# A fixed order table for every engine, input loads in one queue, more zero matmuls at the start, and three key tiles computed without the folded weight

## The chip, the cores and the metric

The kernel runs on one core of a Trainium2 chip. The metric is the device time of one execution in microseconds; smaller is better. The engines are PE (matrix multiply, with its weight loads listed as PEld), DVE (vector), ACT (scalar), POOL (GpSimd) and SP (which here only issues DMAs). All of them work through their own instruction lists in program order and wait for each other by semaphores.

## The reference

A sequence of 2048 tokens of 512 numbers passes through two layers. Each layer is a linear attention with 32 heads of 16 numbers, and then a gated two-matrix block (GLU) with 1376 hidden columns; both have a residual and a layer norm without weights in front, and the two layers use the same weights. Cut to what matters:

```python
q, k, v = split(x @ wqkv)                       # 32 heads x 16
pq, pk = q @ w_phi, k @ w_phi                   # per head, 16 x 16
phi = concat(softmax(p), softmax(-p))           # for q and for k: 32 features
kv, z = sum_s phi_k * v, sum_s phi_k            # per head, over all tokens
o = (phi_q @ kv) / (phi_q @ z + 1e-6);  x = x + o @ wo
gate, up = xn @ W_gate, xn @ W_up
x = x + (gate * (gate > 0) * up) @ W_down
```

The sums kv and z run over all tokens, so every key of a layer must be done before most queries of it can be used.

## The kernel before, in words

The tokens are 16 tiles of 128 rows in four chunks of four tiles. All of X, all weights and all intermediate tiles stay on the chip.

Setup (lines 201 to 292) issues the loads. On SP's queue: the key part of wqkv, X tile 1, X tiles 2 and 3, the value part. On ACT's queue: X tile 0, w_phi, X tiles 4 to 7, 8 to 11, the query part of wqkv, X tiles 12 to 15. Then it makes constants on DVE and POOL.

The rest is a plan. Each helper calls `pl.op(engine, cost, function, reads, writes, ...)`, which only records an operation; at the end `order` gives every operation a place and a buffer, and `emit` issues them in that order. Before, `order` is a list scheduler: a simulated clock, costs and due times (X_IN, WK_IN and so on), and for each group a rank from the table RANK decide which ready operation each engine takes next.

The operations that the change and the prediction touch:

- `wake` (line 312): STEP["wake"] zero matmuls of 512 columns on PE (line 318).
- `feature_weights` (line 322): Wblk is w_phi spread into a block-diagonal matrix (line 327, DVE). The key weight is folded with it: 16 transposes of wkv by PE (line 351), copies out of PSUM, 16 matmuls against Wblk (line 364), copies into Wk2 (`evacuate`, line 307 on ACT or 309 on DVE). The query weight is folded in the same way from DMA transposes (line 337). So keys in feature form are one product of the normalised tile with Wk2, four matmuls of 512 columns.
- `Norm` (line 370): statistics on DVE (lines 388 and 390), the inverse root on POOL (lines 396 and 398, and 446 and 448 where ACT normalises), the normalised tile on ACT (line 460), DVE or POOL (line 472), and then its transpose, which PE or a DMA of SP makes. STEP["turn"] = "A-AA" has tiles 0, 2 and 3 of the first chunk transposed by PE (line 481), and tile 1 by a DMA (line 490). Two tiles that share one DMA transpose are line 486.
- `keys_values` (line 697): keys (line 710), their two exponentials (line 715, ACT), values (line 663), sums of features per head (`feature_sums`: line 682 both signs at once on DVE, line 692 one sign, or line 679 a first addition of halves on POOL and line 688 the rest on DVE), the reciprocal (line 724), the scaling (line 730, a cut in eighths between POOL and DVE), and the sums over tokens (line 752).
- `queries` (line 781) and `attention` (line 821) do the same for queries (lines 794, 798, 682 to 692, 803, 807, 814) and the output projection (line 884).
- `glu` (line 575): the last 96 hidden columns (line 593), gate and up (line 613), their evacuation (619, 623, 626, 630), and down (line 645). A chunk is cut in parts of its four tiles by STEP["part0"] and ["part1"].
- `load_weights` (line 294): the weights of the projection and the GLU, on SP's queue (line 300).

The strings of STEP give for each tile which engine or variant is used.

Of the kernel before, what the change touches and what calls it, by code (L numbers as in the profile page):

```python
# [8 lines left out]
P = 128  # L9
D = 512  # L10
# [3 lines left out]
NDB = D // P  # L14
# [36 lines left out]
TAIL = {"PE": 0.165, "ACT": 0.12, "DVE": 0.115, "POOL": 0.045, "SP": 0.0}  # L51
SAME = {"PE": -0.165, "ACT": 0.035, "DVE": 0.035, "POOL": 0.08, "SP": 0.0}
HOPS = {("DVE", "POOL"): 0.09, ("ACT", "POOL"): 0.15}
NEXT = {"PE": 0.055, "SP": 0.03}
FREE = 0.06


def hop(a, b):
    return SAME[a] if a == b else HOPS.get((a, b), NEXT.get(b, 0.04))


class Plan:
# [10 lines left out]
    def op(self, eng, occ, fn, reads=(), writes=(), holds=(), lat=0.0, at=0.0, group=None, port=False, long=False):  # L73

        o = Op()
        o.eng, o.occ, o.cost, o.fn, o.lat, o.at, o.port, o.long = eng, occ, occ + TAIL[eng], fn, lat, at, port, long
        o.group, o.i_in = group or self.group
        base, slope = RANK.get(f"{o.group}.{eng}") or RANK[o.group]
        o.bias = base - slope * o.i_in
        o.preds, o.succs, o.i = set(), [], len(self.ops)  # L80
# [18 lines left out]
    def order(self):  # L99
        for o in self.ops:  # L100
            for p in o.preds:
                p.succs.append(o)
        for o in reversed(self.ops):
            o.rank = o.cost + o.lat + max([s.rank + hop(o.eng, s.eng) for s in o.succs], default=0.0)
        free = {k: [0.0] * n for k, (pool, n) in self.kinds.items()}
        engines = sorted({o.eng for o in self.ops})
        busy = {e: 0.0 for e in engines}
        ready = {e: [] for e in engines}
        for o in self.ops:
            o.wait, o.t0 = len(o.preds), o.at  # L110
            if not o.wait:
                ready[o.eng].append(o)
        seq, left, now, shut = [], len(self.ops), 0.0, 0.0
        while left:
            moved, later = False, []
            for e in engines:
                if busy[e] > now + 1e-9:
                    later.append(busy[e])
                    continue
                best = None  # L120
                for o in ready[e]:
                    if o.t0 > now + 1e-9:
                        later.append(o.t0)
                        continue
                    if o.port and shut > now + 1e-9:
                        later.append(shut)
                        continue
# [881 lines left out]
```

## Time and profile before

| what | value |
|---|---|
| median of the runs | 382.15 us (380.12 to 382.57, 3 runs) |
| profiled execution | 380.91 us, of it 379.2 us span |
| granted TensorE clock | 0.999 |
| HBM read, written | 8.44 MB, 2.10 MB |

A row of a group gives line, engine, operation, tile written and read, shape and count, then busy time in us and mean ns of one instruction, then the idle time of the engine just before and what ended it. A row in order of time gives start, duration, engine and line; PE's busy time of matmuls is modelled, and matmuls overlap, so the time of a run of equal matmuls divided by their number is their real pace, not the mean of one. Rows of DMA issues give the queue, KB of each and the us from issue to landing.

### The profile page before, as it was taken

What the parts mean: (1) busy time and instruction counts of PE and PEld (TensorE: products, weight loads), DVE (VectorE), ACT (ScalarE), POOL (GpSimd) and SP (SyncE); (2) the same over time, 40 slices, a digit from 0 to 9 for tenths busy, and PEclk for the clock granted to TensorE, in tenths of its full rate; (3) what the DMA queues carried; (4) which work ended last, traced back from release to release, by engine and by line L of the source; (5) the groups of instructions that cost most, each with busy time, mean ns of one, the idle gap of its engine ahead of it and who ended that gap; (6) DMA issues with size and microseconds to landing.
All of it is one profiled execution on the core that took longest, in us unless ns stands there. A gap on an engine that the chain in (4) does not pass through costs nothing.

```text
span 379.2 us, 6724 instructions
## 1 busy us (share of the span) xinstructions
PE 363.6 (96%) x2380; PEld 189.9 (50%) x2409; DVE 268.0 (71%) x608; ACT 205.5 (54%) x439; POOL 121.1 (32%) x203
## 2 busy tenths in 40 slices
PE   4898999999899999999999999999999999999996
PEld 2444545756445444444444456475654445454444
DVE  4999999999925442763497998999962675172433
ACT  4898979776762446737706925865234135514100
POOL 3798965131110220560155681724310002000000
PEclk9999999999999999999999999999999999999999
DMA  8889936788950230021013070478930075000011
GB/s 262 239 143 227 260 44 144 133 149 146 145 107 2 42 58 15 0 30 27 0 22 77 9 119 3 87 127 146 171 85 14 5 146 115 14 0 16 1 55 57
DMA packets 98882, 32.61 MB, mean 86 GB/s; under 512 B 90560, under 2 KB 98336, under 8 KB 98848
## 3 DMA queue, kind: packets, MB, share of 16 engines
q1 hardware_dynamic: 97216, 29.93, 39.7%
q10 hardware_dynamic: 1632, 2.24, 1.8%
q8 instruction: 19, 0.31, 0.4%
q14 instruction: 15, 0.12, 0.1%
HBM read 8.44 MB, written 2.10 MB: 28 GB/s over the span
## 4 chain that ended last, share of the span: by engine, by line
PE 64%; DVE 24%; DMA 6%; issue 2%; ACT 1%; POOL 1%; SPq 0%; POOLq 0%; ACTq 0%
PE ps L613 37%; PE ps L645 14%; PE ps L884 5%; DMA b<-b 4%; DVE sk L682 4%; DVE rk L724 3%; DVE bnst L388 3%; PE ps L794 3%; PE ps L593 3%; DVE sk L692 2%; DVE b L730 2%; PE q L833 2%; DMA X<-in_A_x_dram 2%; DVE sq L682 1%; DVE sk L688 1%
## 5 line engine op out<-in xcount | busy, mean ns | idle before, releaser
L613 PE MATMUL ps<-b,wu 128*128 128x512 bf16 (+2 forms) x400 | 79.2, 336 | 0.6 <-DMA b<-b 0.6
L613 PE MATMUL ps<-b,wg 128*128 128x512 bf16 (+2 forms) x400 | 78.6, 336 | 0.0
L645 PE MATMUL ps<-wd,b 128*128 128x512 bf16 (+3 forms) x368 | 78.1, 366 | 0.3
L623 ACT ACTIVATE b<-ps 128x512 bf16<-128x512 f32 (+2 forms) x100 | 50.5, 520 | 39.6 <-PE ps L613 39.1
L626 DVE SCALAR_TENSOR_TENSOR b<-ps,b 128x512 bf16<-128x512 f32 (+2 forms) x60 | 35.1, 598 | 39.9 <-PE ps L613 38.9
L645 PEld LDWEIGHTS <-b 128*128 128x128 bf16 (+1 forms) x374 | 35.3, 98 | 39.1
L613 PEld LDWEIGHTS <-wg 128*128 128x128 bf16 x400 | 36.1, 98 | 33.1
L613 PEld LDWEIGHTS <-wu 128*128 128x128 bf16 x400 | 36.2, 98 | 32.7 <-issue 0.9
L730 POOL TENSOR_TENSOR b<-b,rk 128x1024 bf16<-128x1024 bf16 (+6 forms) x28 | 37.5, 1351 | 9.6 <-DVE rk L724 7.9
L798 ACT ACTIVATE b<-ps 128x512 bf16<-128x512 f32 x64 | 33.0, 638 | 5.7 <-PE ps L794 5.1
L715 ACT ACTIVATE b<-ps 128x512 bf16<-128x512 f32 x64 | 33.7, 628 | 1.3 <-PE ps L710 1.3
L679 POOL TENSOR_TENSOR b<-b 128x256 f32<-128x256 bf16 x30 | 19.7, 670 | 43.9 <-ACT b L715 34.1
L570 DVE SCALAR_TENSOR_TENSOR X<-ps,r,X 128x512 bf16<-128x512 f32 (+2 forms) x26 | 18.2, 701 | 20.2 <-PE ps L645 20.1
L710 PE MATMUL ps<-Wk,b 128*128 128x512 bf16 x123 | 29.4, 379 | 2.0 <-DMA b<-b 1.2
L884 PE MATMUL ps<-wo,b 128*128 128x512 bf16 x118 | 29.7, 379 | 1.5 <-DMA b<-b 0.9
L630 DVE TENSOR_TENSOR b<-b,b 128x512 bf16<-128x512 bf16 (+2 forms) x40 | 13.5, 348 | 24.0 <-ACT b L623 22.3
L552 POOL TENSOR_SCALAR ve<-tot 128x4 f32<-128x4 f32 x8 | 1.9, 233 | 88.8 <-ACT sq L548 88.8
L663 PE MATMUL ps<-wkv,b 128*128 128x512 bf16 x122 | 29.9, 386 | 0.3
L794 PE MATMUL ps<-Wq,b 128*128 128x512 bf16 x126 | 29.5, 379 | 0.1
L548 ACT ACTIVATE sq<-b 128x512 bf16<-128x512 bf16 x32 | 20.1, 627 | 17.4 <-DVE b L527 17.0
L598 ACT CAST ur<-ps 128x192 bf16<-128x192 f32 (+1 forms) x18 | 5.4, 302 | 32.2 <-PE ps L593 32.1
L814 POOL TENSOR_TENSOR b<-b,rq 128x512 bf16<-128x512 bf16 x19 | 20.2, 1061 | 8.4 <-DVE rq L807 6.1
(94 smaller groups left out, 493.7 us busy)
## 6 DMA issues: line engine op xcount, KB each, us to landing
out_dram<-X SPq DMA_DIRECT2D x15, 128.0 KB, 1.8
X<-in_A_x_dram ACTq DMA_DIRECT2D x3, 512.0 KB, 7.2
b<-b SPq DMA_TRANSPOSE x94, 3.2
wg<-in_B_W_gate_dram SPq DMA_DIRECT2D x8, 160.0 KB, 3.2
wu<-in_B_W_up_dram SPq DMA_DIRECT2D x8, 160.0 KB, 4.0
wd<-in_B_W_down_dram SPq DMA_DIRECT2D x5, 256.0 KB, 4.7
wkv<-in_A_wqkv_dram SPq DMA_DIRECT2D x2, 512.0 KB, 7.1
wq<-in_A_wqkv_dram ACTq DMA_DIRECT2D x1, 512.0 KB, 8.3
```

The costliest lines, as they stand in the source:

```text
L613: nc.tensor.matmul(ps[:], lhsT=wt[:, b, f * P:(f + 1) * P], rhs=xnT[:, lo:hi, b, :], start=(b == 0), stop=(b == NDB - 1))
L623: pl.op("ACT", 0.045 + 0.43 * share, lambda ups=ups, ru=ru, sign=1.0 if fuse else -1.0: nc.scalar.activation(out=ru[:], in_=ups[:], func=A ...
L626: pl.op("DVE", 0.06 + 0.548 * share, lambda gps=gps, ru=ru, h=h, cs=cs: nc.vector.scalar_tensor_tensor(out=h[:, cs], in0=gps[:], scalar=0. ...
L645: nc.tensor.matmul(yps[:], lhsT=hs[f][:fsz, ti * P:(ti + 1) * P], rhs=st.wd[:fsz, f, cols], start=(f == 0), stop=(f == NFT - 1))
L663: nc.tensor.matmul(vp[:], lhsT=xnT[:, ti, kb, :], rhs=st.wkv[:, kb, D:2 * D], start=(kb == 0), stop=(kb == NDB - 1))
L710: nc.tensor.matmul(ps[:], lhsT=xnT[:, ti, kb, :], rhs=w(kb), start=(kb == 0), stop=(kb == NDB - 1))
L715: pl.op("ACT", 0.48, lambda s=s, ek=ek, pk=pk: nc.scalar.activation(out=ek[:, :, s, :], in_=pk[:].rearrange("p (j x) -> p j x", j=8), func ...
L730: eng.tensor_tensor(out=phiK[:, lo:hi, :, :].rearrange("p j s (f h) -> p (j s) f h", h=4), in0=ek[:, lo:hi, :, :].rearrange("p j s (f h) - ...
L794: nc.tensor.matmul(pq[:], lhsT=xnT[:, ti, kb, :], rhs=st.Wq2[:, kb, :], start=(kb == 0), stop=(kb == NDB - 1))
L798: pl.op("ACT", 0.48, lambda s=s, eq=eq, pq=pq: nc.scalar.activation(out=eq[:, :, s, :], in_=pq[:].rearrange("p (j x) -> p j x", j=8), func ...
L814: (nc.vector if on_dve else nc.gpsimd).tensor_tensor(out=e, in0=e, in1=rq[:].unsqueeze(2).to_broadcast([P, 8, DH, 4]), op=Alu.mult)
L884: nc.tensor.matmul(yps[:], lhsT=turned(b), rhs=st.wo[:, b, :], start=(b == 0), stop=(b == NDB - 1))
```

## The change

Six things change together.

1. The list scheduler, its constants and RANK go. `order` takes the operations in the order of a table ORDER of 1912 numbers (operation numbers in program order) and gives each buffer the free slot that was used longest ago. Due times and costs that stay in the calls no longer decide anything.
2. The loads: SP issues X tile 0, X tile 1, the key weight, X tiles 2 and 3, the value weight, X tiles 4 to 7, 8 to 11, the query weight, X tiles 12 to 15, in this order; ACT issues only w_phi. The code of `load_weights` differs only in a planning number.
3. Zero matmuls: 26 and not 3. In ORDER 14 of them are PE's first work; 8 stand between weight transposes and folds, and 4 among the first raw keys.
4. Keys of tiles 0, 1 and 2 of layer 0 are computed in two steps: the transposed keys from the unfolded weight (16 matmuls of 128 columns), a copy out of PSUM to bf16 (ACT, ACT, DVE for the three tiles), and then four matmuls of 128 columns against Wblk. The other tiles keep Wk2.
5. STEP is new as a whole: turn is "----" (no tile of the first chunk is transposed by PE), and the choices of engine for normalising, sums, scaling, evacuation, transposes and parts differ for most tiles.
6. With this the order on every engine differs throughout.

```diff
-WF_IN, WK_IN, WV_IN, WQ_IN, LOADED = 3.4, 4.2, 6.7, 10.4, 11.0
+LOAD_SP = ((0, 1), (1, 2), "k", (2, 4), "v", (4, 8), (8, 12), "q", (12, 16))
+LOAD_ACT = ("f",)
...
+        owner = {k: [None] * n for k, (pool, n) in self.kinds.items()}
+        last = {k: [-1] * n for k, (pool, n) in self.kinds.items()}
+        self.seq = [self.ops[i] for i in ORDER]
+        for at, o in enumerate(self.seq):
...
+            for b in o.bufs:
+                if b.slot is None:
+                    free = [i for i, u in enumerate(owner[b.kind]) if u is None or not u.left]
+                    b.slot = min(free, key=lambda i: last[b.kind][i])
+                    owner[b.kind][b.slot] = b
...
+        if L == "0" and t < STEP["raw"]:
+            kT, kTs = Buf("ps", [P, NDB, P], F32), Buf("b1", [P, NDB, P], BF16)
+
+            def raw(kT=kT, ti=ti):
+                for b in range(NDB):
+                    for kb in range(NDB):
+                        nc.tensor.matmul(kT[:, b, :], lhsT=st.wkv[:, kb, b * P:(b + 1) * P], rhs=xnT[:, ti, kb, :],
+                                         start=(kb == 0), stop=(kb == NDB - 1))
+            pl.op("PE", 16 * TR, raw, reads=[(xnT, ti)], writes=[(kT, 0)], holds=(kTs,), at=WK_IN)
+            evacuate(st, STEP["kev"][t], lambda kT=kT, kTs=kTs: (kTs[:], kT[:]), 0.59, reads=[(kT, 0)], writes=[(kTs, 0)])
+
+            def features(pk=pk, kTs=kTs):
+                for b in range(NDB):
+                    nc.tensor.matmul(pk[:, b * P:(b + 1) * P], lhsT=kTs[:, b, :], rhs=st.Wblk[:, b, :], start=True, stop=True)
+            pl.op("PE", 4 * TR, features, reads=[(kTs, 0), ("Wblk", 0), ("Wblk", 1)], writes=[(pk, 0)], holds=(ek, phiK))
+        else:
...
-    "part0": "4111", "part1": "6111", "tB0": "D---", "tB1": "--DA", "tA": "----", "wev": "ADADAAAAADDAAAAA",
-    "xn1": "ADAADDAPDAADDAAA", "turn": "A-AA", "wake": 3, "fuse0": "AFAA", "fuse1": "FFFF", "gate": 1, "sA": 2,
...
-    "kr0": "11H11HH11H2211H1", "kr1": "H22P11H2111222PP", "qr0": "21H1H11P2PH11212", "qr1": "112H121HH1HPP12P",
+    "raw": 3, "kev": "AADA", "part0": "3111", "part1": "6111", "tB0": "D--D", "tB1": "A--A", "tA": "----",
+    "wev": "AAAAAAAADDADAAAA", "xn1": "ADAPDAADDAAPAAAA", "turn": "----", "wake": 26, "fuse0": "AFFF",
...
+    "om0": "12222222", "om1": "11222222", "ev0": "AAAAAAAAAAAAAAAA", "ev1": "ADDAAADAAAAAADDA",
+    "ks0": "6087550655660860", "ks1": "4661026302258586", "kr0": "2H2P11H11PP21HP1", "kr1": "222PH11P1P1HP112",
```

The first numbers of ORDER are `0 1 2 3 4 5 127 125 134 149 143 140 123 150 141 133 144 142 139 131 129 137 159 8 9`: the statistics and POOL steps of tile 0, then zero matmuls (123 to 148), the two halves of Wblk (149, 150), the first weight transposes (159) and tile 1 (8, 9).

More of the change, by code (lines that the diff above doesn't have):

```diff
@@ L99, in order @@
     def order(self):
[L100 to L112, printed above, removed]
@@ L317, in wake @@
         z = Buf("ps", [P, D], F32)
[L318 removed]
+        pl.op("PE", 0.2155, lambda z=z: nc.tensor.matmul(z[:], lhsT=st.zero[:, 0:P], rhs=st.zero[:], start=True, stop=True),
               writes=[(z, 0)], at=1.2)
```

156 lines of the change are left out of this document (44 added, 112 removed), and 103 rows, old and new, of tables (ORDER, RANK, STEP).

## The prediction

> **What bounds the kernel now.** I read the page first (busy shares and the chain), then busy time by stretches, then the start in order of time.
>
> ```profile
> PE 363.6 (96%) x2380; PEld 189.9 (50%) x2409; DVE 268.0 (71%) x608; ACT 205.5 (54%) x439; POOL 121.1 (32%) x203
> ...
> PE 64%; DVE 24%; DMA 6%; issue 2%; ACT 1%; POOL 1%; SPq 0%; POOLq 0%; ACTq 0%
> ```
>
> PE is nearly always busy and holds 64% of the chain that ended last; DVE holds 24%. The stretches tell where each is true (columns: stretch and length, then busy us of PE, PEld, DVE, ACT, POOL, granted clock, DMA share, GB/s).
>
> ```profile
> 0.00:12.00 12.00, 6.17 (x42) 4.01 (x42) 7.18 (x26) 5.64 (x10) 4.83 (x21) 1.00 0.87 285
> 12.00:60.00 48.00, 45.20 (x330) 22.72 (x337) 48.00 (x100) 43.32 (x85) 40.70 (x55) 1.00 0.77 173
> 60.00:184.00 124.00, 122.03 (x783) 64.29 (x790) 79.92 (x205) 77.09 (x178) 27.79 (x50) 1.00 0.40 71
> 184.00:250.00 66.00, 64.82 (x476) 33.75 (x482) 59.71 (x122) 40.22 (x85) 34.42 (x58) 1.00 0.29 53
> 250.00:350.00 100.00, 99.11 (x617) 52.18 (x620) 62.31 (x142) 37.45 (x83) 13.38 (x21) 1.00 0.39 75
> ```
>
> The first 12 us are a start: PE idles 5.8 us and DVE 4.8. From 12 to 60 DVE has no idle time at all, with PE at 94%, ACT at 90% and POOL at 85%: everything is nearly full and DVE sets the pace. From 60 to 350 PE is the bound and idles 2.0 + 1.2 + 0.9 = 4.0 us in all. So the change can win only at the start, by freeing DVE up to 60, or from those 4 us.
>
> **The start, PE.**
>
> ```profile
> 1.24 1.46 PE L318 MATMUL ps<-zero 128*128 128x512 bf16 x3 [1.24 <-DVE zero L234]
> 5.37 1.89 PE L351 MATMUL ps<-ident,wkv 128*128 128x128 bf16 x16 [2.66 <-DMA wkv<-in_A_wqkv_dram]
> 7.11 1.01 PE L364 MATMUL ps<-Wblk,b 128*128 128x128 bf16 x8
> 10.04 0.61 PE L364 MATMUL ps<-Wblk,b 128*128 128x128 bf16 x4 [1.93 <-DVE b L309]
> 12.00 1.80 PE L663 MATMUL ps<-wkv,b 128*128 128x512 bf16 x4
> 13.63 1.89 PE L710 MATMUL ps<-Wk,b 128*128 128x512 bf16 x7
> ...
> 66.93 0.67 PE ps L613 x12
> ...
> 322.25 16.40 PE ps L613 x76
> ```
>
> The last two rows are the later rate: 56 ns for a pass of 128 columns, 216 ns for 512. The early rows run at about half of it: 118 ns for 128 columns at 5.37, 450 ns for 512 at 12.00, 270 at 13.63. The first work on a token tile is the values matmul at 12.00.
>
> **When the first tile reaches PE afterwards.** This is the step on which the sum turns. The order table, decoded by numbering the operations in program order, puts on PE 14 zero matmuls, then the 16 weight transposes and folds among 8 more zeros, and then the raw keys of tile 0, which wait for that tile transposed. Before, tiles 0, 2 and 3 are transposed by PE (turn "A-AA"); now all go through the DMA queue of SP (turn "----"), and on that queue nine loads stand ahead of them.
>
> ```profile
> 3.86 0.69 DVE L388 BATCH_NORM_STATS2 bnst<-X 128x6 f32<-128x512 bf16 x1 [1.09 <-DMA X<-in_A_x_dram]
> 6.48 0.17 DVE L390 BATCH_NORM_AGGREGATE mv<-bnst 128x2 f32<-128x6 f32 x1
> 8.21 0.82 ACT L460 ACTIVATE b<-X,ve,rstd 128x512 bf16<-128x512 bf16 x1
> 5.34 0.33 ACTq L240 DMA_DIRECT2D X<-in_A_x_dram  x1
> X<-in_A_x_dram ACTq DMA_DIRECT2D x1, 128.0 KB, 3.0
> X<-in_A_x_dram ACTq DMA_DIRECT2D x1, 512.0 KB, 8.1
> ```
>
> (The last two rows are DMA issues with the us from issue to landing.) Tile 0 landed after 3.0 us, at 3.8. From the start of the aggregate to the end of the normalising it is 9.03 - 6.48 = 2.55 us, and the statistics take 0.69. With X first in its row and the aggregate no longer behind the wait for w_phi, the normalised tile stands at about 3.8 + 0.7 + 2.55 = 7.0 us. The nine loads need an issue of 0.45 us each and are all issued by about 5.5, so the transpose is issued behind them at 7. The bytes are the same as before, whose last load landed at 5.34 + 8.1 = 13.4; I take 13.4 again (12.4 if one row is freer of small pieces, 14.6 if one queue is slower than two). Does a transpose pass loads that are ahead of it in its queue?
>
> ```profile
> 17.93 0.43 SPq L300 DMA_DIRECT2D wr<-in_B_W_gate_dram  x1
> 18.95 1.23 SPq L486 DMA_TRANSPOSE b<-b  x1
> wr<-in_B_W_gate_dram SPq DMA_DIRECT2D x1, 96.0 KB, 2.9
> b<-b SPq DMA_TRANSPOSE x1, 4.8
> 34.03 1.23 SPq L337 DMA_TRANSPOSE b<-wq  x1
> wu<-in_B_W_up_dram SPq DMA_DIRECT2D x1, 160.0 KB, 4.0
> b<-wq SPq DMA_TRANSPOSE x1, 4.5
> DMA to landing us min/median/max: 2.7/3.1/4.8
> ```
>
> The transpose at 18.95 follows loads whose last landed at 17.93 + 2.9 = 20.8, and took 4.8 us where the median is 3.1; the one at 34.03 follows a burst of loads (landing in 4.0) and took 4.5. In the two places shown where loads are ahead in the queue the transpose lands after them. Before, the large X parts and wq came through ACT's queue and SP's was nearly empty at 10.7. So I take the first transposed tile 0.9 us behind the last load (a median transpose less its issue and half its tail), at 14.3. The Trainium skill, DMA: Bandwidth & Descriptors, section on queues, rings and completion order, says that each DMA engine consumes the descriptors of a ring in order and that SP and ACT own one row each. By that rule the 14.3 is firm; the traces agree as far as the two places go.
>
> **The sum, against the profiled execution's own 380.9 us** (span 379.2 and 1.7 around it; the median of the runs shown is 382.15, its lowest 380.12).
>
> 1. First tile on PE at 14.3 and not 12.00: +2.3. The same shows on DVE: its table puts the copy of tile 2's raw keys out of PSUM (L309) ahead of the first sum of features. PE reaches the end of those raw keys after three raw tiles, two values and one feature step, 14.3 + 1.9 + 1.8 + 0.4 + 0.9 + 0.9 + 0.9 = 21.1 (half rate for the first 4 us, by the rows at 5.37 and 12.00), so the first sum comes at 21.7 against 19.6 before. That is +2.1, one delay and not two. Take +2.3; bounds -2.8 (tile at 9.2, first rival) and +3.5.
> 2. PE's own work. Three raw tiles cost 16 + 4 passes of 56 ns in place of 4 of 216: +0.25 each, +0.75. Three PE transposes in the first chunk go: -0.67. Later three more attention tiles and one more centred tile are transposed by PE (4 x 4 x 56 ns = +0.9), and chunk 0 of the first GLU is cut in three parts and not two. The 80 further passes cost only their fixed part, by the two rates (4 x 56 - 216) / 3 = 2.7 ns each: +0.2. Together +1.2, all in stages where PE is 94% to 99% busy.
> 3. The 23 added zero matmuls lie in PE's idle time until 8.5 and before raw keys that wait: 0. If the cover goes (tile 0 at 9.2), the four zeros left behind them cost 4 x 0.22 = 0.9.
> 4. Three raw tiles add three copies out of PSUM, two on ACT and one on DVE; ACT loses three copies of turned tiles and gains two of weights: nothing, in ACT's 4.7 idle us.
> 5. DVE up to 100 us.
>
> ```profile
> L682 DVE TENSOR_REDUCE sk<-b 128x64 f32<-128x1024 bf16 x9 | 10.5, 1188 | 0.0
> L688 DVE TENSOR_REDUCE sk<-b 128x32 f32<-128x256 f32 x5 | 2.7, 547 | 0.0
> L472 DVE TENSOR_SCALAR b<-X,mv,rstd 128x512 bf16<-128x512 bf16 x6 | 2.6, 450 | 0.0
> L730 DVE TENSOR_TENSOR b<-b,rk 128x1024 bf16<-128x1024 bf16 x2 | 1.4, 680 | 0.0
> L692 DVE TENSOR_REDUCE sq<-b 128x32 f32<-128x512 bf16 x21 | 13.5, 659 | 0.0
> L814 DVE TENSOR_TENSOR b<-b,rq 128x512 bf16<-128x512 bf16 x13 | 5.7, 445 | 0.2 <-POOL rq L807 0.2
> L679 POOL TENSOR_TENSOR b<-b 128x256 f32<-128x256 bf16 x11 | 7.2, 666 | 1.7 <-ACT b L798 1.4 <-ACT b L715 0.3
> L472 POOL TENSOR_SCALAR b<-X,mv,rstd 128x512 bf16<-128x512 bf16 x1 | 2.1, 2092 | 0.1
> ```
>
> By the new strings of STEP, the keys of layer 0 have six full sums and not nine (-3.5), eleven half sums and not five (+3.2), two normalisings fewer (-0.9), eight more eighths of a scaling (+0.7), two bf16 copies fewer and one f32 copy more (about 0): -0.5. The queries of layer 0 have four full sums fewer (-4.7), five single ones (+3.3) and three half ones more (+1.6), five scalings fewer (-2.2): -2.0. Together -2.5 on the engine that sets the pace; I take -2.0, since part of the queries' share lies behind 60, where PE is the bound. Bounds -2.5 and 0.
> 6. The order past 60. PE idles 4.0 us there, mostly behind transposes. A fixed table can fit them better or worse; no row shows which. Bounds -4.0 and +4.0; I take -2.0, since the new DVE and ACT shares leave the transposes' inputs earlier in the first GLU. What is late next is PE itself.
>
> Sum: +2.3 + 1.2 - 2.0 - 2.0 = -0.5, so 380.9 - 0.5 = 380.4.
>
> The clock at 14.3 is one more unknown. The row at 12.00 shows half rate after a broken start; afterwards PE works from 1.24 to about 9 and then waits 5 us. The Trainium skill, TensorE: Matmul & The Clock Gate, part 1, says that about 3.4 us of idling bring the half rate back. By that rule the zeros warm nothing that lasts, and the sum stays; if PE stayed warm, the first 4 us would be done in 2, and the sum would be 378.4. No row of this trace has a warm PE idle that long.
>
> **The rivals.**
> (a) The transposes are not held up by the loads, and tile 0 is on PE at 7.0 + 2.2 = 9.2. For it: nothing in the first 12 us shows a transpose at all, so the two places above are small cases. Then DVE idles about 3.2 us at the start (until X lands, and for the next parts) where the forecast has 4.8 + 2.1 = 6.9: -3.7, and PE gains 5.1. With 0.9 for the zeros: between 375.3 + 0.9 and 376.7, say 376.
> (b) Slower: POOL becomes the bound of the keys. It is busy 40.7 us of 48 from 12 to 60. It gets six more half-sum additions (6 x 0.67 = 4.0) and a second normalising of 2.1, and loses eight eighths of a scaling (2.0): +4.1, in a stage that starts 2 us later. It decides if more than half of POOL's 7.3 idle us there stay waits; then the stage lengthens by about 4.1 and nothing of step 5 is won: 380.4 + 2.0 + 4.1 = 386.5. Against it: POOL's order is new too, and may wait less.
> (c) The start is as forecast, but the table takes out nearly all of the 4.0 us of PE's idling past 60 and more of DVE's: 380.9 + 2.3 + 1.2 - 2.5 - 4.0 = 377.9.
>
> **How the numbers follow.** Forecast 0.48, its own range 378 to 384; (a) 0.27; (b) 0.15; (c) 0.10. Range 374 to 386.5: (a) with 2 us of margin below, (b)'s price above. A measurement of this kernel can tell about 1% from no change; that is below 378.3 or above 386.0 against 382.15. Faster: most of (a), 0.24, 0.07 of (c), 0.04 of the forecast: 0.35. Slower: 0.10 of (b) and 0.03 of the forecast: 0.13. Within 1%: 0.52.
>
> **What would show it.** Step 1: the first 128-column matmul of raw keys near 14.3, behind a wait for a DMA, and the first transposes of SP with landings of 5 us or more; near 9 it is (a). Step 5: DVE's busy time from 12 to 60 still 48, its first sum near 21.7. Rival (b): waits of PE or DVE for POOL's scaling of keys. Step 6: PE's idle time from 60 to 350 against 4.0. The prediction is wrong if the first tile is early, or if the later order loses by waits what no row here can show.

## The result and the profile after

The kernel after takes 394.41 us (median of 4 runs, 393.69 to 394.76) against 382.36 us for the kernel before beside it: a ratio of 1.032, with a 95% interval of 1.027 to 1.037. The forecast was 380.4, with a range up to 386.5; it was wrong in sign and outside its range. The profiled execution spans 392.8 us, 13.6 more than before. Single executions of 779 to 1381 us (one of the kernel before, one each of two kernels below) are left out of all ratios.

First the same stretches of the kernel after from 12 us on, in the columns used above (stretch, length, busy us of PE, PEld, DVE, ACT, POOL, granted clock, DMA share, GB/s):

```profile
12.00:60.00 48.00, 40.58 (x319) 22.82 (x325) 43.03 (x81) 37.68 (x72) 35.79 (x49) 0.93 0.64 133
60.00:184.00 124.00, 119.22 (x863) 67.20 (x875) 101.05 (x243) 69.95 (x181) 44.41 (x69) 1.00 0.46 86
184.00:250.00 66.00, 63.77 (x411) 31.66 (x415) 48.76 (x88) 28.83 (x54) 28.68 (x47) 1.00 0.23 39
250.00:350.00 100.00, 98.68 (x671) 53.76 (x680) 64.24 (x158) 54.35 (x135) 20.44 (x32) 1.00 0.46 82
```

From 12 to 60 every engine now idles more: PE 7.4 us (before 2.8), DVE 5.0 (0), ACT 10.3 (4.7), POOL 12.2 (7.3), and the clock is 0.93. From 60 to 350 PE idles 8.3 us where it idled 4.0. DVE's idle time lies nearly all in one place, ahead of its first sum of features, where it waits for PE's raw keys of tile 2; the second row is the stretch from that sum to the end of the keys of layer 0:

```profile
23.29 0.69 DVE L239 CAST b<-ps 128x512 bf16<-128x512 f32 x1 [4.21 <-PE ps L648]
```

```profile
23.90:66.07 42.17, 36.18 (x284) 18.76 (x287) 41.41 (x70) 34.10 (x67) 33.54 (x36) 1.00 0.58 127
```

There DVE is busy 41.4 of 42.2 us: it still sets the pace, and PE, ACT and POOL wait.

Where the delay arises is told by fixed places of the program. R is built (before L774, after L720) once the last keys of a layer are summed. These are the rows by line of the kernel before and of the kernel after (duration min/median/max in ns, then the first and the last start in us):

```profile
L774 DVE TENSOR_TENSOR R<-M,q x4: 427/430/439, 52.9 to 233.4; 128x272 bf16<-128x272 bf16 x4
```

```profile
L720 DVE TENSOR_TENSOR R<-M,q x4: 373/424/439, 66.1 to 247.1; 128x272 bf16<-128x272 bf16 x4
```

R of layer 0 is 13.2 us late, R of layer 1 is 13.7 us late, and the span is 13.6 us longer. The whole loss is made before 66 us, in the start and the keys of layer 0; from R on the kernel takes 326.7 us, and 326.3 before. That stage divides at the first sum of features on DVE, at 19.53 before and 23.90 after: 4.4 us are lost ahead of it and 8.8 behind it. Not all of the 8.8 is waiting: the table also does 31 query matmuls ahead of R (7.5 us of PE) where the kernel before did 19 (4.4 us).

The start of the kernel after, PE in order of time, SP's DMA issues, and the us from issue to landing of the last load and of the first transpose:

```profile
10.08 0.83 PE L294 MATMUL ps<-Wblk,b 128*128 128x128 bf16 x8
15.33 1.89 PE L648 MATMUL ps<-b,wkv 128*128 128x128 bf16 x16 [4.42 <-DMA b<-b]
```

```profile
5.31 0.57 SPq L161 DMA_DIRECT2D X<-in_A_x_dram  x1
6.78 7.93 SPq L420 DMA_TRANSPOSE b<-b  x4
```

```profile
X<-in_A_x_dram SPq DMA_DIRECT2D x1, 512.0 KB, 9.5
b<-b SPq DMA_TRANSPOSE x1, 8.5
```

The first transpose is issued at 6.78 and lands 8.5 us later, at 15.3, 0.5 us behind the last load (5.31 + 9.5 = 14.8). PE stands still for 4.4 us, and what it does then goes at half rate (118 ns for each of the 16 passes of 128 columns). The clock, by stretches:

```profile
13.00:14.00 1.00, 0.00 (x0) 0.00 (x0) 1.00 (x3) 0.00 (x0) 0.84 (x4) 0.82 2.37 125
14.00:15.00 1.00, 0.00 (x0) 0.00 (x0) 1.00 (x7) 0.00 (x0) 0.90 (x3) 0.50 0.60 113
```

A mean of 0.82 puts the fall to 0.50 near 13.6, 2.7 us after PE's last matmul ended at 10.9.

Behind the first sum the trace shows something that I had not looked for. The groups of DVE from 15 to 66, scalings of keys and sums:

```profile
L612 DVE TENSOR_REDUCE sk<-b 128x64 f32<-128x1024 bf16 x6 | 7.1, 1181 | 0.0
L618 DVE TENSOR_REDUCE sk<-b 128x32 f32<-128x256 f32 x11 | 6.2, 589 | 0.0
L676 DVE TENSOR_TENSOR b<-b,rk 128x1024 bf16<-128x1024 bf16 x4 | 5.3, 1317 | 0.0
L676 DVE TENSOR_TENSOR b<-b,rk 128x384 bf16<-128x384 bf16 x4 | 3.6, 894 | 0.0
L676 DVE TENSOR_TENSOR b<-b,rk 128x256 bf16<-128x256 bf16 x5 | 2.8, 560 | 0.0
```

The full sums last as long as before (1181 against 1188 ns). A whole scaling (128x1024) takes 1317 ns where the same shape took 680, and 128x256 takes 560. In order of time, DVE first and POOL second:

```profile
47.02 1.38 DVE L676 TENSOR_TENSOR b<-b,rk 128x256 bf16<-128x256 bf16 x1
49.36 0.40 DVE L676 TENSOR_TENSOR b<-b,rk 128x384 bf16<-128x384 bf16 x1
55.51 0.22 DVE L676 TENSOR_TENSOR b<-b,rk 128x256 bf16<-128x256 bf16 x1
56.18 1.94 DVE L676 TENSOR_TENSOR b<-b,rk 128x1024 bf16<-128x1024 bf16 x1
```

```profile
46.98 1.26 POOL L676 TENSOR_TENSOR b<-b,rk 128x640 bf16<-128x640 bf16 x1
55.66 1.91 POOL L676 TENSOR_TENSOR b<-b,rk 128x1024 bf16<-128x1024 bf16 x1 [0.69 <-DVE rk L670]
```

At 47.02 a scaling of 128x256 starts on DVE just after POOL has begun its part of the same tile, and ends 0.16 us after POOL's (48.40 against 48.24); 128x256 with POOL idle, at 55.51, takes 0.22. At 56.18 the same: DVE ends at 58.12, POOL at 57.57. So DVE's scaling does not get on in earnest until POOL's has ended. With 0.68, 0.40 and 0.22 us alone, the 13 scalings of the three shapes would take 4 x 0.68 + 4 x 0.40 + 5 x 0.22 = 5.4 us; they take 11.7. These 6.3 us lie on the engine that paced this stage. POOL waits behind them for DVE's reciprocals, and PE for the scaled keys (us in total, times, longest):

```profile
POOL b L676 <- DVE rk L670: 7.3, 4, 2.4
...
PE q L698 <- DVE b L676: 4.1, 6, 1.5
...
PE q L698 <- POOL b L676: 1.6, 1, 1.6
```

The Trainium skill, SBUF — State Buffer, section on who interferes with whom, calls the pair of ports that DVE shares with GpSimd an exclusive lock: a DVE instruction with two SBUF inputs contends with a GpSimd instruction that reads SBUF, the order of issue decides which of them blocks, and a reduction of DVE never contends. The rows agree: DVE's scaling at 47.02, begun 0.04 us behind POOL's, waits for it, and the full sums keep their length.

Both parts of one tile's scaling wait for the same reciprocal, so they become ready together: a cut scaling collides almost by design unless something keeps the parts apart. The list scheduler had such a rule (by its simulated clock, a `port` operation of DVE is not started while a `long` operation of POOL runs; the variable `shut` in the code before). The table has no rule. The kernel before cuts ten of the 16 tiles of layer 0 as well (`ks0` = "7877011827873780"), so it is not the cutting that is new.

So two causes were proposed, each with rivals: the late first tile (held up by SP's queue, or by the DMA engines being full whatever the queue), and DVE's scalings (held up by POOL, or POOL simply being the bound, or the raw keys, or the zeros, or the order as such).

### The profile page after: what moved, and what is told of

Its sections match the earlier page's. It is cut to its first block, busy times and chain, and to the rows that moved or that the text cites. A ratio compares the mean times of both kernels' runs of the same rounds, so it can differ in the third digit from the quotient of the medians.

```text
span 392.8 us, 6991 instructions
## 1 busy us (share of the span) xinstructions
PE 371.6 (95%) x2529; PEld 200.0 (51%) x2564; DVE 276.6 (70%) x615; ACT 211.5 (54%) x477; POOL 134.9 (34%) x216
## 4 chain that ended last, share of the span: by engine, by line
PE 65%; DVE 27%; DMA 3%; issue 2%; ACT 1%; POOL 1%; DVEq 0%; POOLq 0%; ACTq 0%
PE ps L543 31%; PE ps L575 16%; PE ps L830 5%; DVE b L676 4%; DMA b<-b 3%; DVE sk L612 3%; DVE sq L622 3%; PE ps L523 3%; PE ps L640 2%; DVE rk L670 2%; DVE sk L618 2%; DVE sq L618 2%; DVE sk L622 2%; PE ps L248 2%; DVE b L799 2%
## 5 line engine op out<-in xcount | busy, mean ns | idle before, releaser
L553 ACT ACTIVATE b<-ps 128x512 bf16<-128x512 f32 (+3 forms) x110 | 50.6, 486 | 68.9 <-PE ps L543 68.7
L543 PE MATMUL ps<-b,wu 128*128 128x512 bf16 (+3 forms) x440 | 81.4, 321 | 1.0 <-DVE X L496 0.5
L543 PE MATMUL ps<-b,wg 128*128 128x512 bf16 (+3 forms) x440 | 80.7, 321 | 0.4 <-DVE hr L530 0.2
L575 PE MATMUL ps<-wd,b 128*128 128x512 bf16 (+4 forms) x367 | 78.2, 367 | 0.4
L560 DVE TENSOR_TENSOR b<-b,b 128x128 bf16<-128x128 bf16 (+3 forms) x70 | 21.9, 339 | 36.8 <-ACT b L553 18.5
L549 ACT ACTIVATE b<-ps 128x128 bf16<-128x128 f32 (+3 forms) x70 | 27.5, 424 | 28.0 <-PE ps L543 27.7
L676 POOL TENSOR_TENSOR b<-b,rk 128x768 bf16<-128x768 bf16 (+7 forms) x26 | 35.4, 1371 | 10.3 <-DVE rk L670 8.3
L556 DVE SCALAR_TENSOR_TENSOR b<-ps,b 128x512 bf16<-128x512 f32 x40 | 26.1, 679 | 12.5 <-ACT b L553 7.6
L390 ACT ACTIVATE b<-X,ve,rstd 128x512 bf16<-128x512 bf16 x21 | 16.9, 825 | 16.2 <-POOL ve L378 16.2
L496 DVE SCALAR_TENSOR_TENSOR X<-ps,X 128x512 bf16<-128x512 f32 x32 | 21.5, 677 | 5.6 <-PE ps L830 5.3
```

The source lines that it names most:

```text
L543: nc.tensor.matmul(ps[:], lhsT=wt[:, b, f * P:(f + 1) * P], rhs=xnT[:, lo:hi, b, :], start=(b == 0), stop=(b == NDB - 1))
L553: pl.op("ACT", 0.045 + 0.43 * share, lambda ups=ups, ru=ru, sign=1.0 if fuse else -1.0: nc.scalar.activation(out=ru[:], in_=ups[:], func=A ...
L575: nc.tensor.matmul(yps[:], lhsT=hs[f][:fsz, ti * P:(ti + 1) * P], rhs=st.wd[:fsz, f, cols], start=(f == 0), stop=(f == NFT - 1))
L676: eng.tensor_tensor(out=phiK[:, lo:hi, :, :].rearrange("p j s (f h) -> p (j s) f h", h=4), in0=ek[:, lo:hi, :, :].rearrange("p j s (f h) - ...
```

## Experiments

The kernel before ran beside each group, at 381.96 to 382.29 us. All ratios are to it.

### The late first tile: the queue, or the loads?

**All loads but X tile 0 in ACT's queue**, in the kernel after, so that SP's transposes have only one load ahead of them in their own queue.

```diff
-LOAD_SP = ((0, 1), (1, 2), "k", (2, 4), "v", (4, 8), (8, 12), "q", (12, 16))
-LOAD_ACT = ("f",)
+LOAD_SP = ((0, 1),)
+LOAD_ACT = ("f", (1, 2), "k", (2, 4), "v", (4, 8), (8, 12), "q", (12, 16))
```

> The changed kernel with one edit: SP issues only X tile 0, and all other loads go in the same order through ACT's queue. Theory (the first tiles' transposes stand behind the loads of their own queue): raw keys of tile 0 start on PE at 9.2 to 11.5 us and not 15.3, the first feature sum on DVE near 18 and not 23.9, and the time falls from 394.4 by at least 4, to 386 to 390 if DVE's scalings stay slow (mean 1.3 us for 128x1024), or to about 382 if those collisions come from the late start. Rival (the transposes are slow because the DMA engines are full, whatever the queue): raw keys at 13.5 or later, time 393 to 395.

Measured: 394.96 us, ratio 1.033 (1.028 to 1.037); no change against the kernel after. The rows of this kernel:

```profile
16.05 1.89 PE L648 MATMUL ps<-b,wkv 128*128 128x128 bf16 x16 [5.19 <-DMA b<-b]
```

```profile
5.02 0.52 ACTq L161 DMA_DIRECT2D X<-in_A_x_dram  x1
7.80 6.13 SPq L420 DMA_TRANSPOSE b<-b  x4
```

```profile
X<-in_A_x_dram ACTq DMA_DIRECT2D x1, 512.0 KB, 10.8
b<-b SPq DMA_TRANSPOSE x1, 8.2
```

The transpose is issued at 7.80 with no large load ahead of it in its queue, and lands at 16.0; the last load, in the other queue, lands at 5.02 + 10.8 = 15.8. My reason in step 1 falls: it is not the order of one queue. In both kernels the transpose that is issued while loads fill the DMA engines lands 0.2 to 0.5 us behind the last of them. The Trainium skill, DMA: Bandwidth & Descriptors, section on queues, rings and completion order, says in the same place as the ring order that I leaned on that the write that signals a DMA's end lands only behind all earlier writes of that DMA engine, across its queues. That rule would give both landings, and I had read only half of it; no run here tells it from engines that are simply full.

**The loads of the kernel after in the kernel before**: one queue, same order, nothing else.

```diff
+LOAD_SP = ((0, 1), (1, 2), "k", (2, 4), "v", (4, 8), (8, 12), "q", (12, 16))
...
-    nc.sync.dma_start(out=wkv[:, :, 0:D], in_=wv[:, :, D:2 * D])
-    nc.scalar.dma_start(out=X[:, 0:1, :], in_=xv[:, 0:1, :])
...
+    for what in LOAD_SP:
+        load(nc.sync, what)
+    for what in LOAD_ACT:
+        load(nc.scalar, what)
```

> The kernel before with one edit: its loads are issued as in the changed kernel, all on SP in one row and w_phi alone on ACT. Theory (only what is transposed by DMA suffers): tile 0 is turned by PE and comes sooner, tile 1 and tiles 4 and 5 come by DMA behind the loads, at 14.5 to 15.5; time 382 to 385. Rival (one row of loads is itself slow): the last load lands over 15 us and the time is 387 or more. Rival (loads do not matter): 381 to 383.

Measured: 381.31 us, ratio 0.997 (0.994 to 0.999). Tile 1, whose transpose is issued at 10.29 and takes 4.8 us, lands at 15.1, 0.7 us behind the last load (5.02 + 9.4 = 14.4), as expected; the 382 to 385 us expected with it did not come. One queue for the loads costs nothing; this is the lowest median of the study, 0.3% below the kernel before.

**The first four tiles turned by PE**, at the place in the order where their DMA transposes were issued, with a copy out of PSUM by ACT; the rest as in the kernel after.

```diff
+                if t < 4 and self.at is not None:
+                    tp = Buf("ps", [P, NDB, P], BF16)
+                    def by_pe(xn=xn, ti=ti, tp=tp):
+                        for b in range(NDB):
+                            nc.tensor.transpose(out=tp[:, b, :], in_=xn[:, b * P:(b + 1) * P], identity=st.ident[:])
+                        nc.scalar.copy(out=self.dst[:, ti, :, :], in_=tp[:])
...
```

> The changed kernel with one edit: tiles 0 to 3 are turned by four PE transposes and a copy on ACT, each at the place in the table where its DMA transpose stood. Theory (the late start costs what it shows, 4.3 us at the first feature sum): raw keys start at 9.5 to 11 us and not 15.3, the first sum on DVE at 18 to 20 and not 23.9, no half clock at 15; time 388 to 390.5, with DVE's scalings still at 1.3 us for 128x1024. Second theory (the slow scalings come from the late start, the table being made for an early one): scalings near 0.7 and time 381 to 385. Rival (the stage is bound by DVE and POOL behind it, the start does not count): 393 to 395.

Measured: 390.12 us, ratio 1.022 (1.017 to 1.026).

```profile
12.20 1.05 PE L657 MATMUL ps<-b,wkv 128*128 128x128 bf16 x16 [0.91 <-ACT b L426]
```

```profile
L729 DVE TENSOR_TENSOR R<-M,q x4: 378/426/439, 62.4 to 243.5; 128x272 bf16<-128x272 bf16 x4
```

The raw keys of tile 0 come at 12.20 and not 15.33, at full rate (1.05 us for the 16 passes and not 1.89), and R comes 3.7 us earlier. So the late first tile costs 4.3 us of the 12. DVE's scalings of 128x1024 still take 1317 ns there: they are not slow because the start is late.

### The scalings: POOL's port, or POOL's load?

**A measurement by itself**: DVE scales 128x1024 and 128x256 and then reduces 128x1024 (to its maximum, read in the order in which the kernel sums), over and over; at first alone, then while POOL does 14 scalings of 128x768 on other tiles. It computes nothing of the reference.

```diff
+    for rnd in range(2):
+        for n in range(8):
+            scale(nc.vector, dv[n % 4], ek[0], 0, 8)
+            scale(nc.vector, dv[(n + 2) % 4], ek[0], 0, 2)
+            total(sums[n % 2], ek[0])
+        if rnd == 0:
+            for n in range(14):
+                scale(nc.gpsimd, po[n % 2], ek[1], 0, 6)
```

> Computes none of the reference: it keeps the loads and writes X out, and runs DVE scalings of 128x1024 and 128x256 and DVE sums of 128x1024 first alone and then beside 14 POOL scalings of 128x768. Theory (a DVE scaling waits for the POOL instruction that runs): alone 0.6 to 0.7 us, beside POOL up to 2 us, ending within a scaling's own length after a POOL instruction's end, and the sums unchanged near 1.1. Rival (both only share bandwidth): all DVE operations, sums too, become longer by the same small factor. Rival (no interference; DVE waits for something else in the kernel): 0.7 in both parts.

The rows of DVE, one pair and one reduction alone and then beside POOL (a row of several instructions bears the shape of the first):

```profile
17.29 0.87 DVE L942 TENSOR_TENSOR wg<-wu,Wblk 128x1024 bf16<-128x1024 bf16 x2
18.09 1.20 DVE L946 TENSOR_REDUCE Wk<-wu 128x32 bf16<-128x1024 bf16 x1
...
30.16 2.31 DVE L942 TENSOR_TENSOR wg<-wu,Wblk 128x1024 bf16<-128x1024 bf16 x2
32.40 1.21 DVE L946 TENSOR_REDUCE Wk<-wu 128x32 bf16<-128x1024 bf16 x1
```

The pair takes 0.87 us alone and 2.31 or 2.32 in each of the seven rounds that begin behind POOL's first scaling; the reduction stays at 1.20 to 1.21. So the scaling, with its two inputs, waits for POOL, and the reduction does not. No other kind of DVE instruction was measured.

**No scaling of keys split** between the two engines, in the kernel after: a tile whose cut is 5 eighths or more goes to POOL whole, any other to DVE whole, at the places of the table. Of each line only the call that changes is shown, here and in the two edits of this kind below.

```diff
-scale(nc.gpsimd, 0, cut)
+scale(nc.gpsimd, 0, 8) if cut >= 5 else None
...
-scale(nc.vector, cut, 8)
+scale(nc.vector, 0, 8) if cut < 5 else None
```

> The changed kernel with one edit: no scaling of a key tile is split; where POOL had five eighths or more it does all eight, otherwise DVE does all, at the same places in the table. Theory (DVE waits for POOL's scaling of the same tile, 5.9 us in layer 0 and some more in layer 1): DVE's scalings fall from 11.9 us in layer 0 to under 6, and the time by 3 to 6, to 388.5 to 391.5. Rival (POOL, with 5 us more work, becomes the bound): 394 or more. Start unchanged at 15.3.

Measured: 389.17 us, ratio 1.019 (1.015 to 1.023). 5.2 us are won, although the raw keys still start late, at 14.78. The scalings of DVE up to 66 fall from 11.9 to 5.5 us (four of 128x1024 at 1377 ns).

**Both: PE turns, no split.**

> Both edits at once. If the two causes are separate, the falls add: 383 to 387. If the scalings are slow only because the start is late, no better than the first edit alone. If POOL becomes the bound, as slow as the second edit alone.

Measured: 385.61 us, ratio 1.010 (1.007 to 1.012). The two add up almost fully: 4.3 + 5.2 = 9.5 expected, 8.8 found, of the 12 lost. The first sum is back at 19.26, but R of layer 0 still comes at 59.60, 6.7 us later than in the kernel before; behind R this kernel takes 324.3 us, 2.0 less than the kernel before. Here POOL is full (46.1 us of 48 from 12 to 60), and PE waits once, behind a whole scaling of POOL:

```profile
46.13 0.64 PE L707 MATMUL q<-vext,b 128*128 128x68 bf16 x8 [2.65 <-POOL b L685]
```

```profile
44.16 1.91 POOL L685 TENSOR_TENSOR b<-b,rk 128x1024 bf16<-128x1024 bf16 x1
```

Is POOL's load the bound of what is left, as my rival (b) had it?

**Four more scalings of layer 0 from POOL to DVE** (cut 5; in layer 1 one), on top of both.

```diff
-scale(nc.gpsimd, 0, 8) if cut >= 5 else None
+scale(nc.gpsimd, 0, 8) if cut >= 6 else None
...
-scale(nc.vector, 0, 8) if cut < 5 else None
+scale(nc.vector, 0, 8) if cut < 6 else None
```

> The kernel with turned tiles and whole scalings, and one more move: the four tiles of layer 0 whose cut is 5 are scaled by VectorE and not by GpSimd (in layer 1 the one or two such tiles too). There POOL was busy 46.1 of the 48 us from 12 to 60. If POOL is the bound of what is left (my rival (b), now that VectorE no longer waits for its port), POOL loses 4 x 1.9 us and the time falls by 1 to 3 us, to about 383.5. If the port is still what costs, four more scalings of 0.7 us alone and 1.4 beside POOL come on VectorE: the time rises by 1 to 4 us, to about 388.

Measured: 389.95 us, ratio 1.021 (1.017 to 1.025): 4.4 us slower, with POOL down to 36.9 us from 12 to 60.

```profile
L685 DVE TENSOR_TENSOR b<-b,rk 128x1024 bf16<-128x1024 bf16 x8 | 9.0, 1127 | 0.0
```

POOL's load is not the bound by itself. Eight whole scalings on DVE take 9.0 us and not 5.4: what leaves POOL comes back on DVE with the wait for POOL on top.

**Only tile 9's scaling to DVE**, the one that PE waited for.

```diff
-scale(nc.gpsimd, 0, 8) if cut >= 5 else None
+scale(nc.gpsimd, 0, 8) if cut >= 5 and (L, t) != ("0", 9) else None
...
-scale(nc.vector, 0, 8) if cut < 5 else None
+scale(nc.vector, 0, 8) if cut < 5 or (L, t) == ("0", 9) else None
```

> The kernel with turned tiles and whole scalings, with one scaling moved: that of tile 9 of layer 0 goes to VectorE. TensorE waited 2.65 us for it (43.5 to 46.1) and then did 12 multiplications at half rate, 1.6 us. If that one wait is what is left, the time falls by 2 to 4 us, to about 382.5. If POOL and VectorE are full there and any other tile is late instead, it changes by less than 1 us, or rises as it did when four tiles were moved (by 4.4).

Measured: 384.75 us, ratio 1.006 (1.005 to 1.008), better than without it by 0.9 us between the medians and 0.3% between the ratios, at the edge of what can be told, since the intervals touch; I had expected 2 to 4 us. PE's one wait of 2.65 us became two of 0.78 and 1.15, and the clock fell to half all the same, near 46.6, with PE at work since 46.07: the eight value matmuls at 46.24 take 3.24 us.

**No half sums on POOL** for the keys of layer 0: DVE reduces 128x512 where it reduced the 128x256 that POOL had added up.

```diff
-        pl.op("POOL", 0.62, add, reads=[(e, s)], ...
+        pl.op("POOL", 0.62, (lambda: None) if group == "h0" else add, reads=[(e, s)], ...
...
+                in_=e[:, :, s, :].rearrange("p j (f h) -> p j h f", h=4) if whole else h[:].rearrange("p j f h -> p j h f"),
```

> The kernel with turned tiles and whole scalings, without GpSimd's half sums of the keys of layer 0: VectorE reduces 128x512 bf16 where it reduced 128x256 f32. POOL loses 11 x 0.65 = 7.2 us, VectorE gains 11 x 0.07 = 0.8. If GpSimd's total load sets the end of the keys, the time falls by 2 to 4 us, to about 382.5. If only the place of single scalings counts, it falls by the 0.6 to 1.3 us by which the one scaling that TensorE waited for is earlier, to about 384.7. The last sum is also taken from 64 numbers at once and not from pairs.

Measured: 383.97 us, ratio 1.004 (1.003 to 1.006): better than without this edit by 1.6 us between the medians and 0.5% between the ratios, between what was expected if single scalings count (0.6 to 1.3) and if POOL's total load does (2 to 4).

```profile
L628 DVE TENSOR_REDUCE sk<-b 128x32 f32<-128x512 bf16 x11 | 6.9, 651 | 0.0
```

DVE pays 651 ns a sum in place of 576, 0.8 us in all, for 11 half sums of 0.7 us less on POOL. The wait is not gone from DVE's scalings:

```profile
L686 DVE TENSOR_TENSOR b<-b,rk 128x1024 bf16<-128x1024 bf16 x4 | 5.9, 1476 | 0.0
```

**Both of these edits.**

> Both edits together: tile 9 scaled by VectorE, and no half sums of the keys of layer 0 on GpSimd. If they are two ways to the same wait, the time is that of the better one, about 382. If each frees its own, they add, to about 380.

Measured: 387.75 us, ratio 1.014 (1.012 to 1.016): slower than either alone, which neither expectation had. The trace shows where. With the half sums gone, tile 9's scaling on DVE meets POOL's scaling of the next tile:

```profile
46.23 2.27 DVE L686 TENSOR_TENSOR b<-b,rk 128x1024 bf16<-128x1024 bf16 x1
```

```profile
46.04 6.10 POOL L686 TENSOR_TENSOR b<-b,rk 128x1024 bf16<-128x1024 bf16 x3 [4.65 <-DVE rk L680]
```

```profile
48.55 0.33 PE L708 MATMUL q<-vext,b 128*128 128x68 bf16 x5 [3.87 <-DVE b L686]
```

POOL starts 0.19 us earlier and DVE's 0.68 us become 2.27; PE waits 3.87 us. The five scalings of DVE in that stage take 8.4 us, 5.0 more than alone. A fixed order is a bet on who comes first, and an edit elsewhere turns it.

**The kernel before with its loads in one queue and without those half sums.**

> The kernel before with its loads in one row, without GpSimd's half sums of the keys of layer 0. There GpSimd waits for VectorE and VectorE has no idle time from 12 to 60: five sums become longer by 0.07 us, GpSimd loses 3.3 us that nobody waited for. If VectorE is the bound, as I read it, the time stays or rises by up to 0.5 us, to about 381.6; if VectorE's instructions there are also held up by GpSimd's half sums, it falls by 0.5 to 2 us, to about 380.

Measured: 381.56 us, ratio 0.999 (0.996 to 1.001), as expected of a stage in which DVE is the bound and its rule keeps it clear of POOL.

### The other parts of the change

**The list scheduler back**: all operations and choices of the kernel after, the loads in one queue, ordered by the scheduler and the ranks of the kernel before.

```diff
-ORDER = [int(i) for i in """...""".split()]
+RANK = {
...
-        self.seq = [self.ops[i] for i in ORDER]
+                    if o.port and shut > now + 1e-9:
```

> The changed kernel's operations and choices of engine with the list scheduler and the ranks of the kernel before in place of the table; the loads stay in one row. Theory (the table lets DVE's scalings run beside POOL's long ones, which the scheduler forbids): the mean DVE scaling of 128x1024 falls from 1.3 to about 0.7 us and the total of DVE's scalings in layer 0's keys from 11.9 to about 6, while raw keys still start near 15; time 385 to 389. Rival (the late start explains all of it): scalings stay slow, time 393 to 396. Rival (ranks tuned for other choices do worse than the table): over 396.

Measured: 421.84 us, ratio 1.102 (1.096 to 1.108). The ranks belong to other operations, and with these they order far worse than the table does; this run can't price the table. It does show the rule at work:

```profile
L748 DVE TENSOR_TENSOR b<-b,rk 128x1024 bf16<-128x1024 bf16 x4 | 3.3, 819 | 0.0
L748 DVE TENSOR_TENSOR b<-b,rk 128x384 bf16<-128x384 bf16 x4 | 1.6, 408 | 0.0
```

The same scalings take 819 and 408 ns where the table's order gives 1317 and 894.

**26 zeros in the kernel before**, and **three zeros in the kernel with both edits** (the 23 others left out).

```diff
-    "xn1": "ADAADDAPDAADDAAA", "turn": "A-AA", "wake": 3, ...
+    "xn1": "ADAADDAPDAADDAAA", "turn": "A-AA", "wake": 26, ...
```

> The kernel before with 26 zero matmuls in place of 3, placed by its list scheduler where PE has nothing else. Theory (the zeros keep PE's clock up where PE does not wait long): values at 12.0 take 0.22 us each and not 0.45, the time falls by 0 to 1.5, to 380.5 to 382. Rival (zeros get in the way of weight transposes): 383 or more.

```diff
-        pl.op("PE", 0.2155, lambda z=z: nc.tensor.matmul(...
+        pl.op("PE", 0.2155, (lambda: None) if i >= 3 else lambda z=z: nc.tensor.matmul(...
```

> The kernel with turned tiles and whole scalings, with three zero matmuls and not 26. If the zeros stand ahead of work that waits, as in the kernel before where 23 more cost 3.0 us, the time falls by 1 to 2 us, to about 384. If here, with tile 0 at 12.4 and no long gap in front of it, they keep the clock up, the first 4 us of tile work run at half rate without them and the time rises by 1 to 2 us, to about 387.

Measured: 385.19 us, ratio 1.007 (1.003 to 1.010), and 386.10 us, ratio 1.011 (1.007 to 1.014). In the kernel before the zeros cost some 2.5 us by the ratio: the scheduler puts eight of them where the first values were.

```profile
11.34 1.90 PE L318 MATMUL ps<-zero 128*128 128x512 bf16 x8
...
15.20 1.03 PE L663 MATMUL ps<-wkv,b 128*128 128x512 bf16 x4
```

They do keep PE at full rate (four values in 1.03 us and not 1.80), and the values still start at 15.20 and not 12.00. In the table's order they cost nothing and bring nothing: the ratio without them is within the interval of that with them.

**Raw keys alone in the kernel before**, and **folded keys in the kernel with both edits**.

```diff
+            pl.op("PE", 16 * TR, raw, reads=[(xnT, ti)], writes=[(kT, 0)], holds=(kTs,), at=WK_IN)
+            evacuate(st, STEP["kev"][t], ...)
+            pl.op("PE", 4 * TR, features, ...)
```

> The kernel before, with its list scheduler and its ranks, and only the raw keys of the first three tiles added (the copies out of PSUM on ACT, ACT and DVE). If raw keys bring the features forward, the first sum of VectorE, 19.5 before, comes up to 1 us earlier and the time falls by as much. If they only add work where PE, ACT and DVE are all nearly full, the time rises: 3 x 0.25 us on PE and 0.6 us of copy on DVE, which sets the pace there, so by 0.5 to 1.5 us, to about 383.3; the ranks were not chosen for it, which can add as much again.

```diff
-            pl.op("PE", 4 * TR, features, reads=[(kTs, 0), ("Wblk", 0), ("Wblk", 1)], ...
+            pl.op("PE", 4 * TR, lambda pk=pk, mm=mm: mm(pk, lambda kb: st.Wk2[:, kb, :]), ...
```

> The kernel with turned tiles and whole scalings, but the keys of the first three tiles come from the folded weights, at the place in the order where their features stood; the 16 raw passes, and the three copies out of PSUM, are left out. If the raw keys start the features earlier, the time rises: the folded weights are complete at about 14.6 us, the features of tile 0 stood at 14.4, so by no more than 1 us. If the raw path only costs its own work (0.25 us of PE a tile, two copies on ACT and one on DVE), the time falls by 0.5 to 1.5 us, to about 384.5.

Measured: 393.43 us, ratio 1.029 (1.025 to 1.033), and 385.22 us, ratio 1.008 (1.005 to 1.010). The first can't be read as the price of raw keys: DVE's first sum comes only 0.5 us later than in the kernel before (20.0) while the time is 11 us longer, and 9.3 us of that arise behind R of layer 0 (335.6 us against 326.3), where no raw key is left. That the new operations change what the scheduler picks behind them is the likely reason; it was not tested. I had allowed for 3 us at most. The second leaves the order alone: the intervals with and without raw keys overlap, so these neither cost nor bring anything that can be told.

## Why the prediction was wrong, point by point

**What bounds the kernel.** Right as far as it went: DVE sets the pace from 12 to 60, PE later. The loss sits where DVE was said to have no idle time.

**Step 1** (first tile at 14.3, +2.3) had the right direction and was too small: the tile came 3.3 us late (15.33), inside its bounds of -2.8 to +3.5, because the last load landed at 14.8 and not 13.4. The first sum of DVE came 4.4 us late and not 2.1: 1.0 of the rest is the later tile; the prediction let the half rate end after 4 us, and the trace shows a clock of 0.50 from 13.6 to about 20.5, some 5 us of it under work; and three zeros, put at nothing in step 3, stand between the raw keys that this sum waits for and take 0.43, 0.21 and 0.21 us there. With the tile turned by PE, and so at full rate, the time is 4.3 us shorter. The reason given, the order in SP's queue, was wrong; the kernel with the loads in the other queue shows it. What the prediction took from the Trainium skill, TensorE: Matmul & The Clock Gate, part 1, held: PE idled 4.4 us and the half rate was back, by the rows from 13 to 15, so the zeros warmed nothing that lasts.

**Steps 2, 3 and 4** (PE's own work +1.2, zeros 0, copies 0): with the first tiles turned by PE, the folded keys and the three zeros change nothing that can be told, so zeros and copies stand at 0 there, and of step 2 the 0.75 for raw keys can't be told from 0 either. The rest of step 2 was not tested by itself.

**Step 5 is the step that failed.** It said that the new shares of sums and scalings free DVE by 2.0 us up to 100, by pricing every instruction at its duration in the trace of before. For the scalings that price holds only while POOL does not scale. The row at 680 ns was taken from an order in which a rule kept the two apart; the change takes the rule out. The count of eighths was right: eight more go to DVE, as two more whole tiles (16 eighths) and 23 eighths in cut tiles where there were 31; ten tiles are cut before and after. What was wrong is their price, since nothing keeps a DVE scaling from starting while POOL's runs. In place of -2.0 there are 6.3 us more of DVE's time than the scalings take alone, and about 5 us of the kernel's, as the kernel without cut scalings shows. The diff had it in plain sight: `port=True` and `long=True` stay in the calls, and the code that reads them goes.

**Step 6** (-2.0 past 60) did not come in the kernel after: from R of layer 0 to the end it takes 326.7 us, 0.4 more than before. In the 290 us behind R, PE idles 4.5 us in the kernel before, 6.4 in the kernel after and 3.3 in the kernel with both edits, by these three rows in this order:

```profile
52.90:342.90 290.00, 285.47 (x1874) 150.02 (x1894) 206.53 (x479) 158.55 (x352) 81.79 (x138) 1.00 0.39 72
66.07:356.07 290.00, 283.62 (x1945) 153.59 (x1970) 209.59 (x480) 153.82 (x371) 88.09 (x140) 1.00 0.40 73
59.60:349.60 290.00, 286.67 (x1987) 154.99 (x1986) 207.55 (x477) 155.62 (x375) 87.07 (x135) 1.00 0.40 73
```

The 8.3 us from 60 to 350 also hold 1.9 us from 60 to R, in the keys of layer 0. With both edits the part behind R is 2.0 us shorter than before, which is the size that was forecast; that the number agrees is partly luck, since query work done ahead of R is taken off that part too.

**The rivals.** (a) and (c) fell. (b) named POOL as the cause and had the right place, but its mechanism did not come: POOL is less busy there than before (35.8 us against 40.7) and waits 7.3 us for DVE's reciprocals, while DVE waits inside its own instructions. Such a wait shows in no list of waits; it shows only as a longer duration of the same shape.

**What stays open.** The late tile, the cut scalings and the half sums together bring the ratio from 1.032 to 1.004. The last 1.6 us are not shown. What is open ahead of R is more: in that kernel the stretch from the first sum to R takes 38.9 us, where it took 33.4 before and 42.2 in the kernel after, so of the 8.8 us lost there only 3.3 are given back, and the total looks better because the part behind R is 2.2 us shorter than before. Part of the other 5.5 us is the query work moved ahead of R (33 query matmuls there, 7.8 us of PE, against 19 and 4.4). DVE's four scalings still take 5.9 us, 3.2 more than alone, and PE still waits 1.9 us for POOL; what share these have was not tested. A table made with the rule of the scheduler was not tried.

## What to carry to other kernels

Price an elementwise instruction with two SBUF inputs on DVE by what POOL does at that moment, and do not cut one such operation between the two engines unless the order keeps the parts apart: here a pair of scalings of 0.87 us became 2.31. When a change removes a scheduler, list the rules that it enforced, since durations read from its trace hold only under them. While large loads run, turn the first tile on PE and not by a DMA: here the transpose landed with the last load, whichever queue the loads were in.

## What the runs showed of the hardware

- How long PE may wait before the clock falls can't be read off the length of the wait. PE's last matmul ended at 10.9 in the kernel after and the clock halved near 13.6, 2.7 us later. In the kernel with both edits PE waited 2.65 us from 43.5, and the clock fell within this stretch:

```profile
45.50:46.50 1.00, 0.37 (x7) 0.38 (x8) 0.21 (x1) 0.00 (x0) 1.00 (x2) 0.77 0.89 231
```

  A mean of 0.77 puts the step at 46.04, 2.6 us after the last matmul, and the clock is back at 1.00 from 49.5. The same wait in the kernel with folded keys, 2.67 us, left the clock at 1.00 and the matmuls behind it at full rate:

```profile
45.66 0.43 PE L708 MATMUL q<-vext,b 128*128 128x68 bf16 x8 [2.67 <-POOL b L686]
46.30 1.89 PE L602 MATMUL ps<-wkv,b 128*128 128x512 bf16 x7
```

  In the kernel with no scaling split the clock fell only 4.7 us after the last matmul (10.3 to 15.0), and with tile 9's scaling on DVE it fell after two waits of 0.78 and 1.15 us with 0.65 us of work between them. The Trainium skill, TensorE: Matmul & The Clock Gate, part 1, gives about 3.4 us of idling; these runs show falls on both sides of that. In the kernel with both edits the half rate cost some 1.7 us of PE's time but nothing that shows in the total: its executions at a mean clock of 0.996 take 385.38 to 386.07 us, those at 0.999 and 1.000 385.14 and 385.60.
- POOL's half sums save DVE almost nothing: 128x256 f32 in 576 ns against 128x512 bf16 in 651, for 0.7 us of POOL each (13 of them in 9.0 us).
